# Attention outputs kept as features by tokens and scaled by rows from DRAM, and maxima transposed by VectorE

## The chip, the cores and the metric

One core of a Trainium2 chip runs the whole kernel. The metric is the device time of an execution in microseconds; lower is better. The engines are TensorE (PE, with its weight loads PEld), VectorE (DVE), ScalarE (ACT), GpSimd (POOL) and SyncE (SP), which issues most DMAs; GpSimd issues some. Each engine works through its own instructions in a fixed order, and waits on semaphores for the others.

## The reference

A transformer block over 2048 tokens of 576 features, with 32 heads of 18 features and a conditioned layer norm; all data is float32.

```python
q, k, v = qkv[0], qkv[1], qkv[2]
scores = jnp.einsum("bhqd,bhkd->bhqk", q, k) * scale
p = _softmax(scores, axis=-1)
o = jnp.einsum("bhqk,bhkd->bhqd", p, v)
return (lambda x, *d: x.transpose(*d))(o, 0, 2, 1, 3).reshape(B, S, D) @ wo
...
x = x + ga * _A_ref(h, A_wqkv, A_wo)
h = _layernorm(x, axis=-1) * (1 + cb) + sb
x = x + gb * _B_ref(h, B_w_gate, B_w_up, B_w_down)
```

`_B_ref` is a gated feed-forward net with 4608 hidden features: `(sigmoid(h w_gate) * (h w_up)) w_down`.

## The kernel before

After the projection of q, k and v, attention runs in 32 **units**. Unit u holds a pair of heads p = u % 16 for half = u // 16 of the tokens, 1024 queries. A unit goes through 16 tiles of 128 keys (kt), two at a time: such a pair of steps has eight score matmuls (keys by queries, so a probability tile has the keys on its partitions), eight exponentials on ACT (L1088) and eight value matmuls (L656) that sum up in the accumulator `o`. A column of ones beside the values gives the sum of the probabilities, so `o` holds for each of four (head, 512 queries) a block of 32 partitions: 18 features, and the sum in the 19th.

Softmax subtracts each query's maximum. It comes from a second set of score matmuls (queries by keys, L550), whose results VectorE reduces (L556, L561) and, for a part, ACT helps with (L559). Eight such maxima go with each pair of steps, for a later unit. At the end of a unit's maxima `nm` (L568) holds the negated maxima, 128 queries by 16. `spread` (L577) transposes it on PE (L581), splits it into a high and a low part (ACT L585, VectorE L586), and four DMAs on SP (L590, `q<-mrows`) write it as two more rows of that unit's queries `q`. A score matmul (L1084) reads these rows too, so the first scores of a unit wait for the DMAs. SP also loads the heads of later units (`load_heads`, L514 to L522) at the start of each unit.

`taken` (L668) copies a finished accumulator to `oT`. `outputs` (L676) transposes it on PE in four blocks (L683), copies that back (ACT L699), takes the reciprocal of the sums (VectorE L702), and multiplies on GpSimd (L705) into `Oa` or, for the second half, `big`: tokens by features. `project_o` (L754) then turns each tile of 128 tokens again (L772; L789 for the last 64 features), because the product with wo needs features on the partitions; evacuates it (L778), splits it (GpSimd L779, L780) and multiplies. These parts hang beside the steps of attention: the first half's rows from unit 15 (with loads of wo, layer norm and operand parts behind them, `first_rows`) to unit 27, the second half's from there on. A pair of steps that has such matmuls beside it is called heavy here; the others are light. Features 384 and up of the second half's tokens go to DRAM (`oend`) and are projected after attention in `last_rows` (transposes at L1526 and L1534).

The order of PE and ACT is the order of the program: `STEPS` spells it out for the two steps of a pair by letters (t a score, m and r and x maxima, A/B/V values, K `taken`, G a place for a projection part, O and S the transposes of the outputs and of the maxima). VectorE's, GpSimd's and SP's orders come from a list scheduler that starts from the program's order. On GpSimd, `down_parts` (L939) splits the weights of the down projection from unit 4 to unit 15, in blocks that are tied to the exponentials of the steps (`paced`, L931), so that they don't run ahead.

Of the kernel before, what the change touches and what calls it, by code (L numbers as in the profile page):

```python
# [23 lines left out]
P = 128  # L24
# [63 lines left out]
def tile_block(ctx, tc, x_in, wqkv, wo, w_gate, w_up, w_down, c_in, w_mod, out):  # L88
# [206 lines left out]
    oend = dram.tile([P, 8, D - DL], F32, name="oend")  # L295
# [230 lines left out]
    def maxima():  # L526
# [4 lines left out]
        for u in range(UNITS):  # L531
# [4 lines left out]
            for i in range(8 * n):  # L536
                if last is not None and i == (9 if u == 1 else 8):
                    if u == 1:
                        for _ in spread(*last):
                            pass  # L540
                    else:
                        state["spread"] = last
# [34 lines left out]
    def spread(qs, nm):  # L577

        n = HW // P
        tp = bank()[0 : 2 * n, 0:P]  # L580
        nc.tensor.transpose(tp, nm.rearrange("p h t -> p (h t)"), ident)  # L581
        yield
        mrows = small.tile([32 + 2 * n, P], F32R, name="mrows", bufs=1)
        parts = [mrows[32 * l : 32 * l + 2 * n] for l in range(2)]
        nc.scalar.copy(parts[0], tp)  # L585
        nc.vector.tensor_sub(parts[1], tp, parts[0].bitcast(F32))  # L586
        for h in range(2):
            for l, part in enumerate(parts):
                to = 64 * h + 3 * DH + l
                nc.sync.dma_start(  # L590
                    qs[to : to + 1, :].rearrange("l (t q) -> l t q", q=P).bitcast(F32),
                    part[n * h : n * (h + 1), :].bitcast(F32),
                )
# [40 lines left out]
    Os = [Oa]  # L634
# [33 lines left out]
    def taken():  # L668

        if "whole" in state:  # L670
            half, p, acc = state.pop("whole")
            oT = epool.tile([P, 512], F32, name="oT")
            nc.scalar.copy(oT, acc)
            state["end"] = (half, p, oT)

    def outputs():  # L676

        if "end" not in state:
            return
        half, p, oT = state.pop("end")  # L680
        tp = bank().rearrange("p (b q) -> p b q", q=P)
        for b in range(4):
            nc.tensor.transpose(tp[:, b, :], oT[:, b * P : (b + 1) * P], ident)  # L683

        yield
        tq = tp.rearrange("p b (j e) -> p j b e", e=32)
        rec = epool.tile([P, 4, 4], F32, name="rec")
        if half == 1 and p == H // 2 - 1:
            nc.vector.reciprocal(rec, tq[:, :, :, DH])
            state["last"] = epool.tile([P, 512], F32, name="oT")[:, 0 : 16 * DH].rearrange("p (t e) -> p t e", t=8)  # L690
            for h in range(2):
                nc.vector.tensor_tensor(
                    state["last"][:, :, h * DH : (h + 1) * DH].rearrange("p (c b) e -> p c b e", c=2),
                    tq[:, 2 * h : 2 * h + 2, :, 0:DH],
                    rec[:, 2 * h : 2 * h + 2, :].unsqueeze(3).to_broadcast([P, 2, 4, DH]),
                    op=ALU.mult,
                )
            return
        nc.scalar.copy(oT, tp.rearrange("p b q -> p (b q)"))  # L699
        yield  # L700
        tq = oT.rearrange("p (b j e) -> p j b e", j=4, e=32)
        nc.vector.reciprocal(rec, tq[:, :, :, DH])  # L702
        for h in range(2):
            f0 = (2 * p + h) * DH
            nc.gpsimd.tensor_tensor(  # L705
                Os[half][:, :, f0 : f0 + DH].rearrange("p (c b) e -> p c b e", c=2),
# [1111 lines left out]
```

## Time and profile before

| what | us |
|---|---|
| runs before: median (lowest to highest) of 3 | 2798.32 (2797.94 to 2798.35) |
| the profiled execution | 2804.88 |
| its span in the trace | 2803.1 |
| attention, from the first exponential to the end | 236.1 to about 1531.8 |
| a light unit, u5 | 38.3 |
| four heavy units, u16 to u19 | 183.7 |
| the gate, up and down stages behind attention | 1271 |

The page's first rows give an engine's busy time and its share of the span. In a group of instructions stand: line, engine, operation, output <- input, shapes and count, then the busy time in all, the mean of one in ns, and the idle time before with what ended it. In a timeline row the first number is the start, the second the time until the last of the counted instructions has ended; a row SPq or POOLq is an issue of a DMA. In a window row each engine has its busy time and count, and behind them the granted clock, the mean busy share of the DMA engines and GB/s.

### The profile page before, as it was taken

Reading aid. Unit: us, or ns where it says so; the run is one execution under the profiler, and the core shown is the slowest. Engines: PE = TensorE matmul, PEld = TensorE weight load, DVE = VectorE, ACT = ScalarE, POOL = GpSimd, SP = SyncE. Lnnn points to the kernel's source line nnn. Section 1 sums busy time; section 2 is a strip of 40 time slices with the busy share of each in tenths; the row PEclk is TensorE's granted clock in tenths of the full one; section 3 lists DMA queues with packets and bytes.
Section 4 is the critical chain, followed back from the end, with each engine's and each line's share of the span. In section 5 each row is a group of like instructions: output and inputs, shape, how many; then the busy total and the mean of one; then the engine's idle time right before and its main releaser. Section 6 shows DMA issues by size and latency. Waiting matters only on the chain.

```text
span 2803.1 us, 50644 instructions
## 1 busy us (share of the span) xinstructions
PE 2771.9 (99%) x18637; PEld 1847.4 (66%) x18637; DVE 2306.3 (82%) x4370; ACT 1609.3 (57%) x3051; POOL 814.6 (29%) x1077
## 2 busy tenths in 40 slices
PE   7999999999999999999999999999999999999999
PEld 5975444444444444444444888888888888888888
DVE  7278999999998888999883778888898677777777
ACT  3215999999999878999888332333333222222221
POOL 3125207888843111663103222232221100000000
PEclk9999999999999999999999999999999999999999
DMA  5344224444432120232127766667767956566653
GB/s 172 121 157 140 78 61 162 171 169 166 172 133 82 36 58 24 98 106 71 43 68 227 273 222 223 240 213 273 278 245 280 339 195 201 194 200 195 200 195 120
DMA packets 170777, 462.59 MB, mean 165 GB/s; under 512 B 21212, under 2 KB 88032, under 8 KB 160416
## 3 DMA queue, kind: packets, MB, share of 16 engines
q1 hardware_dynamic: 150064, 360.72, 38.4%
q0 software_dynamic: 20464, 98.62, 9.9%
q8 instruction: 147, 2.41, 0.4%
q14 instruction: 102, 0.84, 0.1%
HBM read 281.92 MB, written 176.82 MB: 164 GB/s over the span
## 4 chain that ended last, share of the span: by engine, by line
PE 92%; DVE 4%; DMA 2%; issue 2%; POOL 0%; ACT 0%; SPq 0%; DVEq 0%; ACTq 0%; POOLq 0%
PE x L1225 26%; PE o L656 19%; PE s L1084 12%; PE s L550 11%; PE d L1375 8%; PE d L1307 6%; PE s L336 4%; PE s L805 2%; PE s L389 1%; DMA out_dram<-Oa 1%; DVE mx L556 1%; PE s L683 1%; DMA wq_raw<-in_A_wqkv_dram 1%; DVE w L1215 0%; DVE Oa L1379 0%
## 5 line engine op out<-in xcount | busy, mean ns | idle before, releaser
L1088 ACT ACTIVATE p<-s 128x512 f32<-128x512 f32 x2048 | 1069.1, 616 | 89.2 <-PE s L1084 62.6
L556 DVE TENSOR_REDUCE mx<-s 128x1 f32<-128x512 f32 x1568 | 1000.9, 683 | 101.3 <-PE s L550 75.1
L656 PE MATMUL o<-p,vaug 128*32 128x256 f32 (+1 forms) x5848 | 595.1, 478 | 0.1
L550 PE MATMUL s<-k,q 54*128 54x512 f32 x1920 | 548.6, 434 | 2.0 <-DVE t L775 1.0
L1084 PE MATMUL s<-q,k 56*128 56x512 f32 x1920 | 527.7, 440 | 0.0
L550 PEld LDWEIGHTS s<-k,q 54*128 54x128 f32 x1920 | 273.4, 184 | 231.9 <-DVE mx L561 88.0
L1084 PEld LDWEIGHTS s<-q,k 56*128 56x128 f32 x1920 | 249.8, 184 | 232.1 <-ACT p L1088 72.9
L1225 PE MATMUL x<-k,w 128*128 128x512 f32 x1512 | 370.0, 392 | 0.0
L1225 PEld LDWEIGHTS x<-k,w 128*128 128x128 f32 x1512 | 276.8, 188 | 53.3 <-PE o L656 0.8
L1375 PE MATMUL d<-wd,hh 128*128 128x288 f32 x1248 | 249.9, 295 | 2.4 <-DVE Oa L1379 2.4
L656 PEld LDWEIGHTS o<-p,vaug 128*32 128x32 f32 x5848 | 116.2, 108 | 203.1 <-issue 187.5
L1225 PE MATMUL x<-big,w 128*128 128x512 f32 x1008 | 245.5, 392 | 0.7 <-DVE u L1724 0.7
L1225 PE MATMUL x<-w,w 128*128 128x512 f32 x1008 | 245.3, 391 | 0.0
L1225 PEld LDWEIGHTS x<-big,w 128*128 128x128 f32 x1008 | 185.1, 188 | 37.0 <-DVE u L1724 1.1
L1225 PEld LDWEIGHTS x<-w,w 128*128 128x128 f32 x1008 | 184.3, 188 | 34.5
L1375 PEld LDWEIGHTS d<-wd,hh 128*128 128x128 f32 x1248 | 202.2, 188 | 6.2 <-DVE Oa L1379 3.1
L1375 PE MATMUL d<-wd,hl 128*128 128x288 f32 x624 | 184.3, 295 | 0.0
L1379 DVE TENSOR_TENSOR Oa<-Oa,d 128x288 f32<-128x288 f32 x312 | 136.6, 453 | 55.1 <-PE d L1375 51.2
L561 DVE CUSTOM_DVE_ANT_0 over<-s,over 128x512 f32<-128x512 f32 x240 | 163.9, 683 | 1.3 <-PE s L1084 1.2
L559 ACT ACTIVATE over<-s 128x512 f32<-128x512 f32 x240 | 145.8, 608 | 11.3 <-PE s L550 9.3
L1234 ACT ACTIVATE sg<-x 128x512 f32<-128x512 f32 x36 | 21.6, 599 | 210.2 <-PE x L1225 210.2
L1206 ACT CAST w<-S 128x768 fp32r<-128x768 f32 x71 | 59.4, 836 | 137.8 <-POOL S L1179 136.0
(275 smaller groups left out, 3898.5 us busy)
## 6 DMA issues: line engine op xcount, KB each, us to landing
ws<-w SPq DMA_DIRECT2D x126, 640.0 KB
w<-ws SPq DMA_DIRECT2D x126, 640.0 KB
wd<-wds SPq DMA_DIRECT2D x19, 1152.0 KB
k<-kd SPq DMA_DIRECT2D x60, 360.0 KB
wds<-w POOLq DMA_DIRECT2D x18, 1152.0 KB, 5.2
wtd<-t POOLq DMA_DIRECT2D x32, 576.0 KB, 5.0
wt<-wtd SPq DMA_DIRECT2D x64, 288.0 KB
wd<-wds SPq DMA_DIRECT2D x52, 288.0 KB
```

What stands on the lines that cost most here:

```text
L336: nc.tensor.matmul(acc, w, hT[:, t, cols], start=n == 0, stop=n == len(ts_) - 1)
L550: nc.tensor.matmul(sp, qs[rows, qt * P : (qt + 1) * P], ks[rows, at * 512 : (at + 1) * 512], start=True, stop=True,)
L556: nc.vector.tensor_reduce(to, sp, axis=AX.X, op=ALU.max)
L559: nc.scalar.activation(over, sp, AF.Relu)
L561: nc.vector.tensor_tensor_reduce(out=over, in0=sp, in1=over, scale=1.0, scalar=LOWEST, op0=ALU.add, op1=ALU.max, accum_out=mx[:, h * n + q ...
L656: nc.tensor.matmul(acc[32 * j : 32 * j + 32, cols], vaug[:, kt, (2 * p + h) * VW : (2 * p + h) * VW + 32], probs[2 * c + h][:, cols], star ...
L1084: nc.tensor.matmul(sT, ks[rows, kcols], qs[rows, c * 512 : (c + 1) * 512], start=True, stop=True)
L1088: state["exp"] = nc.scalar.activation(pr, sT, AF.Exp, scale=SCALE)
L1225: nc.tensor.matmul(acc[v], w[:, v, a, :], X[s][:, b, :], start=first and n == 0, stop=n == 6, skip_group_check=not first,)
L1307: nc.tensor.matmul(acc, a[:, rows], w[:, k, :], start=n == 0, stop=n == 2)
L1375: nc.tensor.matmul(acc[:, :HALF], a[:, f, rows], w[:, f, cols], start=n == 0, stop=n == 5)
L1379: nc.vector.tensor_add(Oa[:, t, cols], Oa[:, t, cols], acc[:, :HALF])
```

## The change

`oT` stays features by tokens. Four small DMAs on SP lay the four rows of sums out as `sT` (128 partitions by 16), VectorE takes the reciprocal of that, one DMA stores it to `osums` in DRAM, and one loads it back as `R`, with each row of 512 repeated on 32 partitions. GpSimd multiplies `oT` by `R` in place, and four DMAs write the 18 features of each block to `ot` in DRAM, 576 features by 2048 tokens. `load_rows` brings tiles of 128 features by 1024 tokens back into `big`, which is then the operand of the projection with wo without a transpose: `project_rows` takes the place of `project_o`, with its splits (`rows_parts`) one tile of tokens ahead on GpSimd. The last unit's accumulator is stored unscaled to `lastd`, and `last_rows` scales it. `spread` splits the maxima first, transposes them with VectorE in blocks of 32x32, and eight DMAs write two rows at a time. The letters O and S leave `STEPS`, and a heavy pair is no longer held back at kt 2 and 12.

```diff
-    2: "V m1t0 t1t0 m0m1 O A c m1r0 t1m0 t1t0 G B c x0t1 m1t0",
-    4: "V r0m1 t1t0 m1m0 G A c t0t1 m1t0 B t1m0 m1t0 t1x0",
-    12: "V t0m1 m0t1 m1t0 S A c r0t1 m1t0 G B c t1t0 m1x0 t1m0",
 }
...
-    oend = dram.tile([P, 8, D - DL], F32, name="oend")
+    ot = dram.tile([D, S], F32, name="ot")
+    osums = dram.tile([UNITS, 4, 512], F32, name="osums")
+    lastd = dram.tile([P, 512], F32, name="lastd")
...
     def spread(qs, nm):
 
         n = HW // P
-        tp = bank()[0 : 2 * n, 0:P]
-        nc.tensor.transpose(tp, nm.rearrange("p h t -> p (h t)"), ident)
-        yield
...
+        split = small.tile([P, 4 * n], F32R, name="split", bufs=1)
+        hi, lo = (split.rearrange("p (h l t) -> p h l t", h=2, l=2)[:, :, l, :] for l in range(2))
+        nc.vector.tensor_copy(hi, nm)
+        nc.vector.tensor_sub(lo, nm, hi.bitcast(F32))
+        mrows = small.tile([P, 4 * n], F32R, name="mrows", bufs=1)
+        nc.vector.transpose(mrows.bitcast(F32), split.bitcast(F32))
+        for a in range(4):
+            for h in range(2):
+                to, p0 = 64 * h + 3 * DH, 32 * a + 2 * n * h
                 nc.sync.dma_start(
-                    qs[to : to + 1, :].rearrange("l (t q) -> l t q", q=P).bitcast(F32),
-                    part[n * h : n * (h + 1), :].bitcast(F32),
+                    qs[to : to + 2, :].rearrange("l (t a q) -> l t a q", a=4, q=32)[:, :, a, :].bitcast(F32),
+                    mrows[p0 : p0 + 2 * n, :].bitcast(F32),
                 )
...
     def taken():
+        if "whole" not in state:
             return
+        half, p, acc = state.pop("whole")
+        oT = epool.tile([P, 512], F32, name="oT")
+        nc.scalar.copy(oT, acc)
+        if half == 1 and p == H // 2 - 1:
+            nc.sync.dma_start(lastd, oT)
+            return
+        sT = epool.tile([P, 16], F32, name="sT")
+        for j in range(4):
+            one = oT[32 * j + DH : 32 * j + DH + 1, :]
+            nc.sync.dma_start(sT[32 * j : 32 * j + 32, :], one.rearrange("l (q r) -> l q r", r=16))
+        follow.append(outputs(half, p, oT, sT))
+
+    def outputs(half, p, oT, sT):
+
+        while state["kt"] < 2:
+            yield
+        rec = epool.tile([P, 16], F32, name="rec")
+        paced(nc.vector.reciprocal(rec, sT))
+        to = osums[half * H // 2 + p]
+        nc.sync.dma_start(to.rearrange("j (q r) -> (j q) r", r=16), rec)
+        R = state["room"] if "room" in state else bgp.tile([P, 512], F32, name="R")
+        nc.sync.dma_start(R, to.unsqueeze(1).to_broadcast([4, 32, 512]))
         yield
+        while state["kt"] < 6:
+            yield
+        paced(nc.gpsimd.tensor_mul(oT, oT, R))
         for h in range(2):
...
+            for c in range(2):
+                f0, n0, j = (2 * p + h) * DH, half * HW + c * 512, 2 * h + c
+                nc.sync.dma_start(ot[f0 : f0 + DH, n0 : n0 + 512], oT[32 * j : 32 * j + DH, :])
...
+    def load_rows(half, tiles):
+
+        own = slice(half * HW, (half + 1) * HW)
+        for i in tiles:
+            if i < 4:
+                nc.sync.dma_start(state["rows"][:, i, :], ot[i * P : (i + 1) * P, own])
+            else:
+                for p0 in (0, 64):
+                    nc.sync.dma_start(state["rows"][p0 : p0 + 64, 4, :], ot[DM:D, own])
+    def rows_parts(t):
...
+        src = state["rows"][:, 0:n, cols]
+        oh, ol = (T[:, a : a + n * P] for a in (0, 512))
+        oh3, ol3 = (a.rearrange("p (i q) -> p i q", q=P) for a in (oh, ol))
+        nc.gpsimd.tensor_copy(oh3, src)
+        nc.gpsimd.tensor_sub(ol3, src, oh3.bitcast(F32))
+        om = None
+        if t < 8:
+            om, omh = bgp.tile([P, P], F32R, name="om", bufs=2), T_[:, 640:768].bitcast(F32R)
+            end = state["rows"][:, 4, cols]
+            nc.gpsimd.tensor_copy(om[0:64], end[0:64])
+            nc.gpsimd.tensor_copy(omh[64:P], end[64:P])
+            nc.gpsimd.tensor_sub(om[64:P], end[64:P], omh[64:P].bitcast(F32))
+    def project_rows(t0):
+
+        ahead = rows_parts(t0)
+        if t0:
+            yield
...
+        for t in range(t0, t0 + 8):
+            n, oh, ol, om, xt = ahead
+            for h in range(2):
...
+                nc.vector.tensor_add(to[:, cols], xt[:, cols], acc[:, 0:HALF])
+                if h == 0 and t < t0 + 7:
+                    ahead = rows_parts(t + 1)
+                if h == 1 and t >= 8:
+                    nc.gpsimd.dma_start(x1p[:, t - 8, :], xt)
...
-        for t in range(8):
-            yield from project_o(t)
+        yield from project_rows(0)
...
+        if u in (14, 26):
+            state["big"] = big.tile([P, 8, 640], F32, name="big").rearrange("p a b -> p (a b)")
+            state["rows"] = state["big"].rearrange("p (i n) -> p i n", n=HW)
+            if u == 26:
+                state["room"] = state["big"][:, 4 * HW : 4 * HW + 512]
+            load_rows(u // 26, range(3) if u == 14 else range(2))
...
-                hold = heavy and (kt == 2 or kt == 12 and u < UNITS - 1)
-                halved = step >= 10 and (hold or not heavy)
+                halved = step >= 10 and not heavy
...
-                elif does in "OSG":
-                    if halved and kt == 2:
-                        follow.append(outputs())
-                        next(follow[-1], None)
+                elif does == "G":
                     if "spread" in state:
-                        follow.append(spread(*state.pop("spread")))
-                        next(follow[-1])
-                    if does == "G" and step >= FROM0 and not hold:
+                        spread(*state.pop("spread"))
+                    if step >= FROM0:
                         state["next"] = next(rows0 if step < FROM1 else rows1, None)
...
+            if (u, kt) == (15, 9):
+                load_rows(0, (3,))
+            if (u, kt) == (16, 7):
+                load_rows(0, (4,))
+            if (u, kt) == (27, 7):
+                load_rows(1, (2,))
...
+                c = t0 // 4
+                n0 = HW + 512 * c
+                od = pool.tile([P, 2, 512], F32, name="od")
+                nc.sync.dma_start(od[:, 0, :], ot[DL:DM, n0 : n0 + 512])
...
+                for p0 in (0, 64):
+                    p1 = p0 + 64 - 2 * DH
+                    nc.sync.dma_start(end[p0:p1], ot[DM : D - 2 * DH, n0 : n0 + 512])
+                    for h in range(2):
+                        j, p2 = 2 * h + c, p1 + h * DH
+                        nc.sync.dma_start(end[p2 : p2 + DH], lastd[32 * j : 32 * j + DH, :])
+                        nc.sync.dma_start(R[p2 : p2 + DH], to[j : j + 1, :].to_broadcast([DH, 512]))
...
+                nc.vector.tensor_mul(end, end, R)
```

The lists below are the instruction order of an engine in the compiled program; names are tiles, and a number behind x counts like rows in a run.

SP in unit 4 and around it. Before, with the maxima's rows as `mrows`:

```order
L518 DMA k_2233<-kd 36x1x2560
L522 DMA k_2233<-kd 18x2560
L198 DMA gates<-w_4052 1x288 x2
L199 DMA gb_b<-gates 128x576
L590 DMA q_1029<-mrows 1x8x128 x4
L514 DMA q_1021<-qd 36x1x1024
```

The same engine now, in unit 5; `sT` are the sums, `ot` the outputs in DRAM:

```order
L521 DMA k_2242<-kd 18x2560
L677 DMA sT<-oT 32x1x16 x4
L687 DMA osums<-rec 128x16
L689 DMA R<-osums 128x1x512
L697 DMA ot<-oT 18x512 x4
L587 DMA q_1027<-mrows 2x8x32 x8
L513 DMA q_1031<-qd 36x1x1024
L516 DMA q_1031<-qd 18x1024
L517 DMA k_2236<-kd 36x1x2560
L521 DMA k_2236<-kd 18x2560
```

The rows of maxima stood alone among loads, and now stand behind the seven DMAs of the outputs, whose last four wait for GpSimd's product.

GpSimd in unit 5, where `w` and `t` are tiles of the down weights and `wtd` their place in DRAM. Before:

```order
L992 DMA wtd<-t_5478 128x1152
L990 CAST t_5479<-t_5479 128x288
L943 DMA w_5793<-in_B_w_down_dram 128x2x576
L991 TENSOR_TENSOR t_5479<-t_5479 128x288
L992 DMA wtd<-t_5479 128x1152
L964 TENSOR_TENSOR w_5443<-w_5443,gb_b 128x288 x3
L973 TENSOR_TENSOR t_5836<-w_5443 128x288
L960 CAST w_5443<-w_5443 128x288 x2
```

And now, at the same place:

```order
L979 DMA wtd<-t_5524 128x1152
L977 CAST t_5525<-t_5525 128x288
L930 DMA w_5848<-in_B_w_down_dram 128x2x576
L978 TENSOR_TENSOR t_5525<-t_5525 128x288
L979 DMA wtd<-t_5525 128x1152
L693 TENSOR_TENSOR oT<-oT,R 128x512
L951 TENSOR_TENSOR w_5492<-w_5492,gb_b 128x288 x3
L960 TENSOR_TENSOR t_5891<-w_5492 128x288
```

The product of the outputs stands between two blocks of the down weights; the two products of L705 of that unit stood ahead of the first of them.

VectorE now, near the end of a light unit's maxima; `mx` are maxima, an ISA row with a tile `over` is the two-input maximum:

```order
L685 RECIPROCAL rec<-sT 128x16
L554 TENSOR_REDUCE mx_1042<-s_4985 128x1
L554 TENSOR_REDUCE mx_1042<-s_4988 128x1
L554 TENSOR_REDUCE mx_1042<-s_4999 128x1
L554 TENSOR_REDUCE mx_1042<-s_5016 128x1
L559 ISA over,mx_1042<-s_5023,over 128x512
L559 ISA mx_1042 128x1
L554 TENSOR_REDUCE mx_1042<-s_5034 128x1
L566 TENSOR_REDUCE nm<-mx_1042 128x16
L580 CAST split<-nm 128x2x8
L581 TENSOR_TENSOR split<-nm,split 128x2x8
L554 TENSOR_REDUCE mx_1041<-s_5047 128x1
```

The reciprocal stood a pair of steps after the copy of `oT` (L699) before; it now stands six maxima ahead of `nm`, and the split of the maxima directly behind it. The transposes of `split` (L583) follow four reduces later.

More of the change, by code (lines that the diff above doesn't have):

```diff
@@ L538, in maxima @@
                     if u == 1:
-                        for _ in spread(*last):
-                            pass
+                        spread(*last)
                     else:
@@ L748, in load_wo @@
         weights.extend((wo_h, wo_l, we))
[L749 removed]
+        for _ in range(6):
             yield
     held_rows = []
[L754 to L810 removed]
@@ L995, in down_parts @@
                     yield
-    def last_rows_project():
-        for t in range(8, NT):
-            yield from project_o(t)
     def load_block(pool, b, k, tied=None):
@@ L1133, in tile_block @@
     taken()
-    for _ in outputs():
-        pass
     manual.close()
-    nc.sync.dma_start(oend[:, :, D - DL - 2 * DH :], state["last"])
     att.close()
@@ L1518, in last_rows @@
             nc.gpsimd.dma_start(w, wod)
[L1519 to L1526 removed]
+            sT = pool.tile([P, 16], F32, name="sT")
```

160 lines of the change are left out of this document (40 added, 120 removed).

## The prediction

> **What bounds the kernel now.** First the page: busy shares, then the chain that ended last.
>
> ```profile
> span 2803.1 us, 50644 instructions
> PE 2771.9 (99%) x18637; PEld 1847.4 (66%) x18637; DVE 2306.3 (82%) x4370; ACT 1609.3 (57%) x3051; POOL 814.6 (29%) x1077
> PE 92%; DVE 4%; DMA 2%; issue 2%; POOL 0%; ACT 0%; SPq 0%; DVEq 0%; ACTq 0%; POOLq 0%
> ```
>
> PE is busy for 99% of the span, but that is an average over stages. So next come the windows: one light unit of attention (u5, no projection beside it), four heavy ones (u16 to u19, with project_o), the two matmul pairs of one t of project_o in u18 and the whole t of four pairs, one t in u29, and all that follows attention.
>
> ```profile
> core 0: us, PE busy (x) PEld busy (x) DVE busy (x) ACT busy (x) POOL busy (x), PEclk, DMA share, GB/s
> 435.33:473.61 38.28, 38.28 (x329) 16.53 (x329) 35.66 (x68) 37.43 (x77) 28.78 (x47) 1.00 0.56 196
> 856.72:1040.38 183.66, 182.97 (x1413) 87.34 (x1405) 158.09 (x314) 151.59 (x300) 34.19 (x62) 1.00 0.17 50
> 962.18:968.70 6.52, 6.52 (x50) 3.54 (x46) 4.91 (x10) 4.65 (x11) 0.00 (x0) 1.00 0.00 0
> 968.70:975.66 6.96, 6.92 (x51) 3.58 (x47) 5.66 (x12) 5.11 (x10) 0.86 (x2) 1.00 0.09 15
> 962.18:986.11 23.93, 23.70 (x182) 11.66 (x178) 20.47 (x42) 18.72 (x38) 3.78 (x7) 1.00 0.05 14
> 1419.13:1436.65 17.52, 17.00 (x127) 7.88 (x125) 15.19 (x29) 13.97 (x27) 1.12 (x2) 1.00 0.11 37
> 1531.80:2803.00 1271.20, 1262.77 (x6946) 1112.96 (x6942) 1017.48 (x1901) 355.20 (x567) 173.94 (x172) 1.00 0.66 228
> ```
>
> In the light unit ACT is busy 37.4 of 38.3 us and VectorE 35.7: these two set it, and PE's "busy" is full because matmuls wait inside it. In the heavy units and after attention the work of PE itself does. So what leaves PE is worth its time in heavy pairs and at the end, and little in light pairs.
>
> **What is removed.** The groups by line, and under them one line of the up stage:
>
> ```profile
> L683 PE MATMUL s<-ident,oT 128*128 128x128 f32 x128 | 20.9, 286 | 0.1
> L699 ACT COPY oT<-s 128x512 f32<-128x512 f32 x31 | 20.5, 662 | 0.0
> L585 ACT CAST mrows<-s 16x128 fp32r<-16x128 f32 x32 | 7.7, 239 | 0.0
> L586 DVE TENSOR_TENSOR mrows<-s,mrows 16x128 fp32r<-16x128 f32 x32 | 9.0, 280 | 4.4 <-ACT mrows L585 3.4
> L702 DVE RECIPROCAL rec<-oT 128x16 f32<-128x16 f32 x31 | 7.8, 252 | 15.8 <-ACT oT L699 15.4 <-issue 0.4
> L705 POOL TENSOR_TENSOR Oa<-oT,rec 128x144 f32<-128x144 f32 x32 | 13.1, 431 | 97.8 <-DVE rec L702 97.6
> L780 POOL TENSOR_TENSOR t<-t,t 128x384 fp32r<-128x384 f32 x4 | 4.0, 1010 | 0.3
> ...
> L1526 PE MATMUL d<-ident,od x8: 272/272/273, 1559.9 to 1624.2; 128*128 128x128 f32 x8
> ```
>
> In a light unit ACT loses L699 and L585, 0.9 us. VectorE loses L586 (0.28) and gets a copy, a subtraction and a 32x32 transpose of 16 or 32 columns; the trace has no such transpose, so I price the three by the small rows here, 0.22 to 0.28 each: +0.4 to +0.6 us. VectorE, already close, then holds the unit at about 38.0: **-0.3** (bounds 0 and -0.9, all of ACT's share). Over the eleven light units without a new wait (u1 to u4, u14, u15, u21, u22, u24 to u26): -3.5.
>
> Heavy pairs: a t of project_o took 23.93 us for four pairs, two of them with transposes only; the new form has two matmul pairs a t (6.52 and 6.96 here; the longer one holds transposes' evacuations beside it) and frees two, which fall back to a light pair's 4.75 (38.28 / 8). 8 x (2 x 6.5 + 2 x 4.75) = 180.0 against the 186.3 that the same 32 pairs took (u16 pair 3 to u20 pair 2): **-6** (bounds -2.5 with the mean of the two, 6.74, and -10 with 6.25 for it if the evacuations' waits go as well). The second half's 17.52 for three pairs, 5.84 each, becomes 2 x 5.84 + 4.75 = 16.43: -8.7 at most for eight, of which I take **-3**, as three of the eight t run beside held pairs. Five more units are in part PE's (u0, u22, u23, u30, u31) and lose 4 x 0.286 of L683 and 0.28 of L581, 1.4 us each: -7 at most, **-4** taken, as about half of their pairs are light. After attention the eight transposes of L1526 and as many of L1534, 272 ns each, leave a stage that PE bounds: **-4** (0 to -4.4), with new small DMAs on SP hidden behind the up and gate work. Sum of the gains: **-20.5**.
>
> **What is added: the row chain on SP.** Now the question is what is late next. SP issues in program order, and the first listing of the change shows its order in a unit: sT, osums, R, four stores of ot, and only then the eight mrows, which the next unit's first scores read. The first ot store waits for GpSimd's product. Before, four issues of mrows followed VectorE and nothing stood ahead of them:
>
> ```profile
> 387.19 2.75 SPq L590 DMA_DIRECT2D q<-mrows  x4
> 395.57 2.06 ACT L1088 ACTIVATE p<-s 128x512 f32<-128x512 f32 x4
> 458.90 0.22 DVE L568 TENSOR_REDUCE nm<-mx 128x16 f32<-128x64 f32 x1
> L198 SPq DMA_DIRECT2D gates<-w x4: 221/229/252, 325.1 to 403.6; - x4
> 406.31 0.36 SPq L199 DMA_DIRECT2D gb_b<-gates  x1
> 330.54 0.35 SPq L199 DMA_DIRECT2D ga_b<-gates  x1
> ```
>
> The issues took 0.69 each and ended at 389.94; the next unit's first exponential ran at 395.57, so there was room. In the new order, with m the time in the unit at which the product starts: 1.28 for the product (L857 below), four stores x 0.65, eight rows of which the last starts 7 x 0.69 later, 1.75 until it has landed (no row shows it: an estimate, two thirds of the 2.7 that the gates below took until a load could follow, since this store ends on the chip), and 0.72 from first score to first exponential. So a unit can't be shorter than **m + 11.2** (1.28 + 2.6 + 4.85 + 1.75 + 0.72). A unit of 38.2 needs m at or below 27.0.
>
> What sets m? First R. By the third listing five reduces and one two-part maximum stand between RECIPROCAL and nm, 3.4 to 4.0 us (0.22 to 0.28 for the small rows is not among them; a reduce is 0.683 by its group below, a little less where they overlap); nm ran at 458.90, u5 + 23.6, so the reciprocal runs at 19.6 to 20.3. Then the store to DRAM and the load that waits for it: the last gates store was issued at 403.6 and the load that waits for it went at 406.31, 2.7 us later; with 0.25 for the reciprocal and 2.3 to 2.8 for the load of R, R is there at u + 24.9 to 26.1. That just fits, with one or two microseconds to spare.
>
> Second, GpSimd's own order. The second listing shows that in u5 the product stands behind the whole block of the down weights up to L992. In the trace of before the row behind which it stands ran here, in u5 to u13:
>
> ```profile
> 435.33 1.08 ACT L1088 ACTIVATE p<-s 128x512 f32<-128x512 f32 x2
> 468.54 0.56 POOL L992 DMA_DIRECT2D wtd<-t  x1 [0.30 <-POOL t L991]
> 502.41 0.59 POOL L984 DMA_DIRECT2D wds<-w  x1
> 540.35 0.42 POOL L990 CAST t<-t 128x288 fp32r<-128x288 f32 x1
> 578.96 0.56 POOL L992 DMA_DIRECT2D wtd<-t  x1 [0.30 <-POOL t L991]
> 623.06 0.72 POOL L943 DMA_DIRECT2D w<-in_B_w_down_dram  x1 [2.15 <-DMA wds<-w]
> 659.67 0.81 POOL L991 TENSOR_TENSOR t<-t 128x288 fp32r<-128x288 f32 x1
> 693.33 0.56 POOL L992 DMA_DIRECT2D wtd<-t  x1 [0.30 <-POOL t L991]
> 737.68 0.56 POOL L992 DMA_DIRECT2D wtd<-t  x1 [0.30 <-POOL t L991]
> 770.66 0.59 POOL L984 DMA_DIRECT2D wds<-w  x1
> ```
>
> Units start 38.3 apart from 435.33, so these rows end at 33.8, 29.4, 28.9, 29.4, 35.1, 33.5, 28.6, 34.6 and 29.4 in their units: 282.7 in all. Less 0.8 each, since the two products of L705 are gone: 282.7 + 9 x (11.2 - 0.8) = 376.3 against 9 x 38.3 = 344.8. In u6 and u13 one row stands ahead of the stores, -0.7 each. That makes **+30** (bounds 0, if GpSimd catches up, and +38, if its blocks also shift). While PE waits there, ACT and VectorE wait with it, and nothing covers it.
>
> The same in u23, where the product is listed behind an operand part of the normalised rows:
>
> ```profile
> 1258.79 1.28 POOL L857 TENSOR_TENSOR t<-t 128x512 f32<-128x512 f32 x1 [0.70 <-DVE t L917]
> 1278.21 0.56 POOL L854 DMA_DIRECT2D xs<-ho  x1
> ```
>
> That stretch took 20.0 us. In the new order it starts behind a transposed block some 18.6 into the unit, so m = 38.0 after the removed work, the unit 49.2 against about 40.2: **+9** (bounds 0 and +12). I place that block by the order, behind four pairs of 4.65. In u27 the first projection waits for rows of ot that SP loads behind the stores (L744). By the order it stands behind 6.5 pairs of 4.9, at 31.8; the stores are issued by 26.1 + 1.3 + 2.6 = 30.0, half a megabyte at the light unit's 196 GB/s takes 2.7 and 1.75 to land, GpSimd's copy and subtraction (L780) 0.5 + 1.0: 35.9, **+4** (0 to +6). u16 by the same reading **+2.3** (0 to +4), u15 +0.3. Sum of the waits: +46.
>
> **Sum.** 46 - 20.5 = **+25.6 us**: 2804.88 of the profiled execution becomes 2830.5. The runs' median, 2798.32, lies 6.6 us below that execution, and the prediction is a median: 2798.3 + 25.6 = **2824**.
>
> **The rivals.** GpSimd's waits from 435 to 830 decide the first:
>
> ```profile
> POOL w L943 <- DMA wds<-w: 37.3, 16, 6.4
> POOL w L964 <- ACT p L1088: 20.5, 8, 4.3
> ```
>
> (a) *GpSimd reaches the product in time*: 37.3 us of its holes wait for its own stores, not for attention, and a unit that is stretched hands it that time; if m stays below 27.0 in u5 to u13, u23 and u27, all 46 us go and the gains stay: 2798.3 - 20.5 = 2778, faster. Against it: eight blocks of the sixteen start only when an exponential lets them (20.5 us), so they shift with the units. The point of decision is m = 27.0. (b) *R itself is late in every light unit*: the other gates, first issued at 325.1, could be loaded only at 330.54: 5.2 us after the second store, in place of 2.7. With 2.5 more, 1.0 of it covered, eleven light units get 1.5 each: 2841; with the sums' first load and store as slow too, 2862. I give it 2848. The light unit's row shows DMA engines busy at 0.56, the heavy ones' 0.17, which speaks for slow trips just there. The Trainium skill, "DMA: Bandwidth & Descriptors", section "Latency and other measured facts", says that reaching DRAM takes 0.2 us on average and 2 us under high load; by that figure, as an estimate, two trips could add 3.6 us a unit, and eleven units at 2.6 beyond the cover would give 2853. The two waits in this trace, 2.7 and 5.2, agree with such a spread, and no run here shows it with its load. (c) *GpSimd catches up in part*: with 2.3 us less before each product (37.3 / 16) the nine units lose 9 x 2.3 = 21 of their 30, and 25 stand against -20.5: 2803, no change.
>
> **How the numbers follow.** Chances: forecast 0.60 (own range 2808 to 2840), a 0.15, b 0.16, c 0.09. A measurement of this kernel tells apart about 0.2%, 5.6 us. Slower: 0.60 and 0.16, less a little: 0.74; same 0.09; faster 0.17. The range leaves out a and the top of b: 2792 to 2856.
>
> **What would show it.** In the changed profile SP's waits name GpSimd's oT before the ot stores; ACT's exponentials pause just at the starts of u6 to u14 and u24, released by PE's scores, and PE's scores by the DMA of mrows; units there are 39 to 45 us, u1 to u4 and u14 near 38. Heavy pairs run one after the other at 6.5, and the chain's share of L683 is gone. Wrong would be: units of 38 in u5 to u13 (a), or 39.5 in all light units with R as the releaser of GpSimd (b).

## The result, and the profile after

| | us |
|---|---|
| runs after: median (lowest to highest) of 4 | 2892.69 (2888.06 to 2894.94) |
| runs before beside them: median of 4 | 2798.13 (2795.52 to 2798.35) |
| ratio, with its 95% interval | 1.0338 (1.032 to 1.0356): slower |
| span of the profiled execution, before and after | 2803.1 and 2885.9 |

Slower, as forecast, but by 94.6 us in place of 25.6. The page after, its first rows, the granted clock and the chain:

```profile
span 2885.9 us, 51086 instructions
PE 2774.4 (96%) x18397; PEld 1833.7 (64%) x18397; DVE 2305.5 (80%) x4406; ACT 1593.9 (55%) x2988; POOL 831.0 (29%) x1048
...
PEclk9999999998988999999999999999999999999999
...
PE 82%; DVE 5%; DMA 4%; POOL 4%; issue 2%; SPq 2%; ACT 0%; DVEq 0%; POOLq 0%; ACTq 0%
```

PE is idle for 4% of the span, GpSimd, DMAs and SP stand on the chain, and the clock has holes in the part where the down weights are split. The groups removed are gone, 240 matmuls fewer, and yet PE's busy time is no smaller (2774.4 us against 2771.9); the rest is in waits. By stage, from the first exponential of each unit (us):

| | start | u0 | u1-u4 | u5-u13 | u14-u15 | u16-u20 | u21-u26 | u27-u31 | rest |
|---|---|---|---|---|---|---|---|---|---|
| before | 236.1 | 43.0 | 156.3 | 344.8 | 76.6 | 230.9 | 236.1 | 208.0 | 1271.3 |
| after | 233.5 | 41.1 | 161.5 | 403.4 | 95.4 | 234.8 | 241.7 | 208.9 | 1265.6 |

Of the 82.8 us between the two spans, 58.6 lie in u5 to u13 and 18.8 in the two units behind. One such unit, u5: SP's, GpSimd's and ACT's timeline of the changed kernel around its end. A name in brackets is what the engine waited for, with the idle time:

```profile
474.40 1.83 SPq L697 DMA_DIRECT2D ot<-oT  x4
476.33 5.38 SPq L587 DMA_DIRECT2D q<-mrows  x8
...
470.64 0.72 POOL L930 DMA_DIRECT2D w<-in_B_w_down_dram  x1 [2.69 <-DMA wds<-w]
...
473.07 1.30 POOL L693 TENSOR_TENSOR oT<-oT,R 128x512 f32<-128x512 f32 x1
...
483.03 1.81 ACT L1071 ACTIVATE p<-s 128x512 f32<-128x512 f32 x3 [7.99 <-PE s L1067]
```

The product starts 37.0 us into u5 (436.1), behind the block of down weights; SP holds the stores and, behind them, the eight rows; u6's first exponential comes 9.96 after the product's start, 7.99 of it as idle time of ACT. So the mechanism of the forecast is there. What it did not have is in PE's clock over the same place:

```profile
476.00:478.00 2.00, 0.00 (x0) 0.00 (x0) 0.00 (x0) 0.00 (x0) 2.00 (x4) 1.00 0.19 46
478.00:480.00 2.00, 0.00 (x0) 0.00 (x0) 0.00 (x0) 0.00 (x0) 2.00 (x5) 0.60 0.02 3
480.00:482.00 2.00, 0.00 (x0) 0.00 (x0) 0.00 (x0) 0.00 (x0) 1.92 (x4) 0.50 0.02 3
482.20:484.20 2.00, 1.97 (x8) 0.97 (x12) 0.48 (x1) 1.05 (x2) 2.00 (x4) 0.50 0.18 50
484.20:486.20 2.00, 2.00 (x16) 0.54 (x10) 0.57 (x2) 0.95 (x3) 2.00 (x4) 0.50 0.49 113
486.20:488.20 2.00, 2.00 (x16) 0.99 (x14) 1.73 (x4) 0.96 (x3) 2.00 (x5) 0.50 0.90 307
488.20:490.20 2.00, 2.00 (x16) 0.59 (x14) 1.20 (x3) 1.97 (x4) 1.69 (x3) 0.89 0.95 270
```

Behind each engine's busy time stands the granted clock. PE's last matmul ended by 474.6; some 4 us later the clock falls to 0.50, and it is back only some 6 us after PE has work again. In that stretch the first pair of u6 takes 7.29 us, where it takes 4.33 behind no wait. Over all of attention the mean granted clock is 0.96, where it was 1.00. The Trainium skill, "TensorE: Matmul & The Clock Gate", section "Part 1: The HAM clock gate", says that PE falls to half its clock after an idle window of about 3.4 us and is released after as long a busy one; the fall here, behind an idle time of 7.8 us, agrees, the way back took nearly twice that.

And VectorE's split of the maxima, in the changed kernel's rows of that line, and at its worst place in u2:

```profile
L580 DVE CAST split<-nm x32: 165/176/5217, 208.9 to 1576.7; 128x16 fp32r<-128x16 f32 x32
...
337.33 5.22 DVE L580 CAST split<-nm 128x16 fp32r<-128x16 f32 x1
342.59 0.17 DVE L581 TENSOR_TENSOR split<-nm,split 128x16 fp32r<-128x16 f32 x1
...
337.04 2.77 POOL L140 TENSOR_TENSOR big<-big 128x576 f32<-128x576 f32 x2
339.77 2.75 POOL L140 TENSOR_TENSOR big<-big,w 64x576 f32<-64x576 f32 x2
```

A copy that takes 0.17 us takes 5.22 while GpSimd runs four operations in a row, and ends with the last of them. That is a second thing that the forecast did not have.

### The profile page after: what moved, and what is told of

The parts are those of the page before. It is cut to its first block, busy times and chain, and to the rows that moved or that the text cites. A ratio compares the mean times of both kernels' runs of the same rounds, so it can differ in the third digit from the quotient of the medians.

```text
span 2885.9 us, 51086 instructions
## 1 busy us (share of the span) xinstructions
PE 2774.4 (96%) x18397; PEld 1833.7 (64%) x18397; DVE 2305.5 (80%) x4406; ACT 1593.9 (55%) x2988; POOL 831.0 (29%) x1048
## 4 chain that ended last, share of the span: by engine, by line
PE 82%; DVE 5%; DMA 4%; POOL 4%; issue 2%; SPq 2%; ACT 0%; DVEq 0%; POOLq 0%; ACTq 0%
PE x L1209 27%; PE o L652 15%; PE s L1067 10%; PE s L548 8%; PE d L1359 8%; PE d L1291 6%; PE s L335 3%; PE s L791 2%; DVE mx L554 2%; PE s L388 1%; DMA wds<-w 1%; SPq L587 1%; POOL w L951 1%; POOL w L948 1%; DMA q<-mrows 1%
## 5 line engine op out<-in xcount | busy, mean ns | idle before, releaser
L1067 PE MATMUL s<-q,k 56*128 56x512 f32 x1920 | 549.2, 451 | 70.1 <-DMA q<-mrows 50.8
L652 PE MATMUL o<-p,vaug 128*32 128x256 f32 (+1 forms) x5848 | 610.0, 488 | 0.2 <-ACT oT L670 0.2
L548 PE MATMUL s<-k,q 54*128 54x512 f32 x1920 | 566.7, 447 | 0.0
L1067 PEld LDWEIGHTS s<-q,k 56*128 56x128 f32 x1920 | 258.1, 190 | 337.9 <-issue 123.7
L548 PEld LDWEIGHTS s<-k,q 54*128 54x128 f32 x1920 | 283.2, 189 | 219.7 <-DVE mx L559 66.2
```

The lines of the kernel that those rows point to most:

```text
L548: nc.tensor.matmul(sp, qs[rows, qt * P : (qt + 1) * P], ks[rows, at * 512 : (at + 1) * 512], start=True, stop=True,)
L652: nc.tensor.matmul(acc[32 * j : 32 * j + 32, cols], vaug[:, kt, (2 * p + h) * VW : (2 * p + h) * VW + 32], probs[2 * c + h][:, cols], star ...
L1067: nc.tensor.matmul(sT, ks[rows, kcols], qs[rows, c * 512 : (c + 1) * 512], start=True, stop=True)
```

## The experiments

The kernel before took 2797.5 to 2799.4 us beside these runs, as the median. e2 and e3 were run once, the others four times or more. Units are the distances of first exponentials, from ACT's rows.

**e1: the stores of ot on GpSimd's queue**, so that SP has nothing that waits for the product.

```diff
-                nc.sync.dma_start(ot[f0 : f0 + DH, n0 : n0 + 512], oT[32 * j : 32 * j + DH, :])
+                nc.gpsimd.dma_start(ot[f0 : f0 + DH, n0 : n0 + 512], oT[32 * j : 32 * j + DH, :])
```

> The changed kernel, but the four stores of ot a unit are issued by GpSimd, behind its own product; nothing on SP waits for the product any more. Theory A (the maxima's rows wait on SP behind the stores that wait for GpSimd): u5 to u15 and u23 fall from 41 to 52 us a unit to 37.8 to 38.5 and PE's waits for q<-mrows go; the clock that PE loses after such a wait comes back too; 2892.7 - 61 (u5 to u13) - 19 (u14, u15) - 9 (u23, u24) = about 2803. The waits of u16 and u27 for rows of ot stay. Rival B (the rows are late by themselves: eight small DMAs, or R through DRAM): the units stay at 41 to 48 and the time above 2870.

2853.24 us, ratio 1.0204 (1.0182 to 1.0225): 39 faster than the change, and far from the 2803 of A. PE's waits in attention, of the change and then of this run:

```profile
PE s L1067 <- DMA q<-mrows: 50.8, 10, 11.2
```

```profile
PE s L1067 <- issue: 18.4, 1, 18.4
PE o L652 <- ACT oT L670: 16.1, 3, 7.1
PE s L1067 <- DVE mx L554: 14.9, 12, 3.7
```

The wait for the rows is gone, as A says, and u5, u7, u8, u11, u12, u14 take 37.7 to 38.7. But the product is still late, and its lateness comes out elsewhere: ACT's next copy into `oT`, of which there is one, waits for the stores that read it (u6 46.2, u13 47.2). In u15 SP's load of `big<-ot` stands ahead of three of the rows and waits for the stores; u9 and u10 take 43.5 and 44.5, where VectorE's split is held for 3.5 and 4.0. So the place on SP was one part of the matter; the late product itself was another. A second buffer for `oT` was not tried.

**e2: the high part by a second reduction.**

```diff
-        nc.vector.tensor_copy(hi, nm)
+        nc.vector.tensor_reduce(hi, mx.rearrange("p (h t) c -> p h t c", h=2), axis=AX.X, op=ALU.max, negate=True)
```

> The changed kernel, but the high part of the maxima is written by a second reduction of mx in place of a copy of nm. In the changed kernel that copy took 0.17 us where GpSimd was idle and 5.22 in u2, where it ended with the fourth of four GpSimd operations in a row; the reduction nm itself never took over 0.25. Theory A (this kind of copy is held while GpSimd computes, a reduction isn't): the row of L580 takes about 0.2 everywhere and u2 is 5 us shorter, unless the subtraction behind it is held for as long. Rival B (any small operation there is held, by something else in u2): the reduction takes 5 us in u2 too. The whole time: 2885 to 2893 by A, unchanged by B.

2871.13 us. The reduction took 0.21 everywhere. In u2 it was the subtraction behind it that now took 5.12, so u2 stayed at 46.35. So the hold is not of one instruction but of a kind: A holds, with the subtraction held in the copy's place. The subtraction has two inputs in SBUF. The time lies below the 2885 to 2893 of A; why u5 to u13 came to 387.0 in place of 403.4, a single run does not tell.

**e3: late rows in the kernel before.**

```diff
+    HOLD = {6: 4, 7: 8, 8: 12, 9: 16, 10: 20, 11: 6, 12: 10}
...
+        for _ in range(HOLD.get(late["u"], 0)):
+            nc.sync.dma_start(spare[late["n"]], parts[1][0:n, :].bitcast(F32))
+            late["n"] += 1
```

> The kernel before, with 4, 8, 12, 16, 20, 6 and 10 extra stores of 4 KB on SP between the first and the second of the four rows of maxima of u6 to u12; 0.63 us each, so 2.5, 5.0, 7.6, 10.1, 12.6, 3.8 and 6.3 us later rows; about 3.8 us of that had room. Nothing else is changed. Theory A (a wait of PE at a unit's start costs itself and a lower granted clock behind it): u6 and u11 stay at 38.3; u7, u12, u8, u9, u10 wait 1.2, 2.5, 3.8, 6.3, 8.8; behind a wait of about 3 us and more the first pair of the next unit is some 3 us longer than 4.36 with a granted clock of 0.5, behind the short ones it isn't. Rival B (the long first pairs of the changed kernel come from its loads of the next heads, late behind the rows on SP, or from its new orders): here too those loads are late, but no granted clock falls, or the first pairs grow with the lateness of the loads also where PE hardly waited.

2818.23 us. The stores were quicker than thought, 0.35 to 0.71 us each in the mean of a unit, so the lateness is less. PE's waits in this run, and the clock in two-microsecond windows behind the longest (at the start of u11, with 20 stores in u10):

```profile
PE s L1091 <- DMA q<-mrows: 10.5, 5, 6.1
```

```profile
676.50:678.50 2.00, 1.88 (x11) 0.70 (x11) 0.69 (x1) 1.62 (x3) 0.00 (x0) 0.50 0.52 176
680.50:682.50 2.00, 2.00 (x16) 0.84 (x9) 1.66 (x4) 1.25 (x3) 0.00 (x0) 0.50 0.58 195
682.50:684.50 2.00, 2.00 (x14) 0.68 (x14) 0.69 (x2) 1.40 (x3) 0.51 (x1) 0.75 0.56 176
684.50:686.50 2.00, 2.00 (x20) 1.06 (x18) 1.88 (x3) 1.91 (x4) 2.00 (x4) 1.00 0.16 44
```

PE waited 2.96 us at the start of u10 and 6.11 at that of u11; both times the clock fell to 0.50, and the first pairs took 8.79 and 8.08 us, against 4.36. The waits at u7 and u9, 0.86 and 0.63 us, left the clock at 1.00. The heads' loads behind the rows come later here too, but no wait of PE names one; so the long first pairs go with the clock: PE waited 10.5 us, u5 to u13 grew by 20.2 (365.0 against 344.8). In this run the waits cost about twice their length.

**e4: the maxima alone**, in the kernel before: `spread` of the changed kernel, all else as it was.

```diff
-                        follow.append(spread(*state.pop("spread")))
-                        next(follow[-1])
+                        spread(*state.pop("spread"))
```

> The kernel before with the new way of the maxima alone (split, 32x32 transposes by VectorE, eight DMAs); the outputs stay tokens by features. Theory A (this part is not what costs): ACT loses 0.24 us a unit and PE a transpose, VectorE gets about 0.3; 2790 to 2800, u2 some 5 us longer if the copy is held there by GpSimd as in the changed kernel. Rival B (the eight DMAs of 128-byte pieces make the rows late): light units above 38.3 with PE waiting for q<-mrows, 2815 or more.

2826.19 us, ratio 1.0101 (1.0084 to 1.0118): +28.7, and neither theory as it was put. No unit waits for the rows. The loss is VectorE's: u2 46.1, u22 46.7 and u25 44.5, which took 39.7, 40.3 and 39.8 before, and u5 to u13 +7.6. Part of it is again the clock: behind PE's waits in u2, u22 and u25 (3.9, 4.1 and 1.6 us) it stood at 0.50 for 6.8 us each.

```profile
L581 DVE CAST split<-nm x32: 160/175/4216, 210.0 to 1508.0; 128x16 fp32r<-128x16 f32 x32
L582 DVE TENSOR_TENSOR split<-nm,split x32: 161/175/3530, 210.2 to 1508.2; 128x16 fp32r<-128x16 f32 x32
```

**e5: the outputs alone**: the changed kernel with `spread` as before.

> The changed kernel with the maxima's rows made as before (PE transpose, ACT copy, VectorE subtraction from PSUM, four DMAs); the outputs stay features by tokens. Theory A (two separate losses: the outputs' product late on GpSimd, some 75 us, and the maxima's split held on VectorE while GpSimd computes, 28.7 us when the maxima are changed alone): 2892.7 - 28.7 = 2864, up to 15 us less since four rows are issued in place of eight behind the product (2.8 us a late unit); u2 falls from 46.6 to about 39; u15 and u16 stay above 50. Rival B (the losses are one, and the outputs alone cost nothing or gain): 2780 to 2810.

2862.45 us, ratio 1.0231 (1.0217 to 1.0246), as A put it (2864). u2 is back at 39.6; u15 takes 49.9 and u16 53.2. Each against the kernel before beside it, the two halves cost 28.7 and 63.0, together 91.7 of the 94.6: they nearly add up.

**e6: the product ahead in GpSimd's order.** On e5: each later operation of the down weights, of wo, of the rows' and the operand parts is tied behind the last product.

```diff
+    def behind(op):
+
+        if "mul" in state:
+            tc.add_manual_dep(
+                op.ins, state["mul"].ins.name,
...
-                nc.gpsimd.tensor_copy(hi[:, quads[i]], raw[:, quads[i]])
+                behind(nc.gpsimd.tensor_copy(hi[:, quads[i]], raw[:, quads[i]]))
```

> As the run with the outputs alone, and GpSimd's later parts (down weights, wo, operand parts) are tied behind the product once the product is written, so that the product stands ahead of them in GpSimd's order; R still comes at 27 us in a unit, and GpSimd waits for it. Theory A (the stall is the product's place in GpSimd's order): the product starts at 27 to 28 us in u5 to u13, u15 and u23, these units take 37.5 to 38.5, PE's waits for q<-mrows go and the granted clock is back at 0.99; the time falls to 2780 to 2800, less what GpSimd's blocks lose by their wait (if they run late, u15 and u16 pay: up to 2815). Rival B (the rows are late through R, the DMAs or SP's crowding): units stay at 41 and more, above 2840.

2837.64 us, ratio 1.0139 (1.012 to 1.0157), above A's range and just below B's. u5 and u9 take 37.7, u15 37.9 in place of 49.9. But GpSimd waits 8.2 us for R in u5 and lacks that time afterwards: the product starts at 36.3 in u7, 34.6 in u10, 33.0 in u11. A product that waits for an R that is there at 27, on an engine that is nearly full, comes late elsewhere.

**e7: the sums early.** On e6: `load_heads(u + 2)` is written behind kt 1.

```diff
-        if 0 < u < UNITS - 2:
-            load_heads(u + 2)
...
+            if kt == 2 and 0 < u < UNITS - 2:
+                load_heads(u + 2)
```

> As the run with the product ahead, and the loads of the heads of unit u + 2 are written behind kt 1, so that SP issues the sums' small DMAs sooner and VectorE takes the reciprocal about 28 rows earlier, near 10 us in the unit; R is there near 16. Theory A: GpSimd no longer waits long for R, its blocks are on time, the rows of ot for u16 and u27 are there in time: 2770 to 2785, faster than both kernels. Rival B (the later loads of the heads make the maxima of unit u + 2 wait, which read them from pair 5 on): light units of 40 and more with PE waiting for k<-kd or q<-qd.

2809.76 us, ratio 1.0033 (1.0021 to 1.0045): 28 better, yet slower than before and above A's range. From u3 on the products start at 18 to 27, and no unit waits for the rows any more. VectorE waits in their place: its reciprocal stands so early that the sums are not there.

```profile
DVE rec L697 <- DMA sT<-oT: 21.5, 9, 5.1
```

**e8: the maxima alone, split from PSUM.** On e4: the maxima are reduced into a PSUM bank and split from there.

```diff
-            nm = small.tile([P, 2, n], F32, name="nm")
+            nm = bank()[:, 0 : 2 * n]
+            nc.vector.tensor_reduce(nm, mx, axis=AX.X, op=ALU.max, negate=True)
...
+            nc.vector.tensor_copy(hi, nm)
+            nc.vector.tensor_sub(lo, nm, hi.bitcast(F32))
```

> The run with the maxima alone, except that the negated maxima are reduced into a PSUM bank and split from there, so that the copy has no SBUF input and the subtraction only one. Theory A (VectorE's copy and subtraction are held because they read SBUF while GpSimd computes): both rows take 0.16 to 0.30 us everywhere, u2 is back from 46.1 to about 39.5 and u5 to u14 from 39.1 to 38.0 to 38.3; 2826.2 - 28.7 = about 2797, between 2790 and 2802. Rival B (the 32x32 transposes, the eight DMAs or the wider rows cost the time): 2815 and more. Rival C (the wait is at the output in SBUF, not at the inputs): the two rows stay long, 2820 to 2826.

2818.26 us, ratio 1.0072 (1.0059 to 1.0086). The rows of the two lines, the copy and the subtraction:

```profile
L571 DVE CAST split<-s x32: 165/174/176, 205.6 to 1499.6; 128x16 fp32r<-128x16 f32 x32
L572 DVE TENSOR_TENSOR split<-s,split x32: 164/165/175, 206.4 to 1499.8; 128x16 fp32r<-128x16 f32 x32
```

No hold is left, u2 takes 39.95, and u5 to u13 346.7 in place of 352.4; with u22 and u25 that is 20.7 us less than in e4. So the hold is of inputs in SBUF; the output `split` lies there in both. The time did not follow (A put 2797), since PE now waits for VectorE to read the bank: u16 to u20 grow from 230.3 to 240.7, and one pair of u18 takes 10.2, where e4 has 5.6. PE in that pair, and the clock behind it:

```profile
980.56 1.11 PE L769 MATMUL s<-ident,Oa 128*128 128x128 f32 x4 [1.59 <-DVE split L572]
...
980.33:983.74 3.41, 3.18 (x16) 1.42 (x16) 1.11 (x5) 0.23 (x1) 1.12 (x2) 0.50 0.03 7
983.74:987.16 3.42, 3.42 (x20) 1.23 (x22) 2.31 (x5) 2.35 (x6) 0.76 (x1) 0.50 0.02 3
```

So here a wait of 1.6 us was enough for 6.8 us at half the clock.

**e9: all mended**: the changed kernel with the split from PSUM, the ties and late heads' loads of e6 and e7, and, in most units, the reciprocal at kt 6 and the product at kt 8.

> The changed kernel with the split from PSUM, the heads' loads behind kt 1, the reciprocal written at kt 6 and the product at kt 8 (two kt sooner in u16 and u27), and GpSimd's later parts tied behind the product. Theory A (the product's place, the sums' late chain, the held split and the lost clock are the whole loss): no unit waits for the maxima's rows, light units take 37.7 to 38.0, u17 and u18 52.0 and 51.1, granted clock 0.99 or more; 2809.8 of the run before it less 22 (its pair 2 waits for the sums) less some 8 (PE transposes in heavy pairs): 2770 to 2785, faster than both kernels. Rival B (something else in the new form costs, such as crowded DMAs): above 2800 with light units over 38.5.

2814.99 us, ratio 1.0068 (1.0055 to 1.008): A's number missed. u5, u6, u13, u14 take 37.7, but in u7 to u12 the product starts at 27.3 to 33.4 and u5 to u13 take 359.8; behind u30, which grew to 42.6, PE waited 7.4 us for the rows. How much of the rest is the PSUM bank's, as in e8, stays open.

**e10: the sums between.** On e7: the reciprocal at kt 4, and VectorE's maxima (split in SBUF) only where GpSimd has little beside them, in u16 to u18 and from u27.

```diff
-        while state["kt"] < 2:
+        while state["kt"] < 4:
...
+                        if 16 <= u <= 18 or u >= 27:
+                            spread_dve(*state.pop("spread"))
```

> The run with the sums early, but the reciprocal is written at kt 4, some six rows later in VectorE's order (it waited 21.5 us in all for the sums there, at 7.7 to 10.8 us in a unit), and in u16 to u18 and from u27 on, where GpSimd had nothing beside it, the maxima are split and transposed by VectorE in place of PE. Theory A (what was left in that run were VectorE's wait for the sums and PE transposes in heavy pairs): pair 2 of u5 to u14 is back at 4.65, -20; u17 at 52 and u28 at 47, -8: 2809.8 - 28 = about 2782, faster than the kernel before by 10 to 18. Rival B (GpSimd's blocks are late then and the product with them): units of 39 to 43 somewhere in u5 to u14, 2795 to 2805.

2785.78 us, ratio **0.9961 (0.9947 to 0.9974): faster than the kernel before**, by 12.5 us, near A's 2782. The window of u5 to u13, of the change and then of this run:

```profile
436.11:839.52 403.41, 362.00 (x2879) 148.97 (x2876) 327.71 (x622) 335.75 (x659) 285.40 (x444) 0.92 0.48 166
```

```profile
429.83:772.82 342.99, 341.43 (x2893) 145.62 (x2894) 321.38 (x604) 333.05 (x668) 272.84 (x422) 1.00 0.55 186
```

Nearly the same GpSimd work (272.84 us in place of 285.40) fits in 60 us less, with the clock at 1.00. All of these units but u7 take 37.7 to 37.8; in u7, 41.0, the reciprocal waits 1.7 us, PE 1.6 behind it, and the clock falls for 3.4.

## Why the prediction was right and wrong

The direction, the chain of waits on SP and the place in GpSimd's order were right. The forecast of 2824 was wrong in its size. Put the gains at the forecast's 20.5, and the 82.8 between the spans leaves about 103 us of losses where 46 were forecast. (The waits as listed add up to 45.6; the half microsecond does not matter.)

- *The gains, -20.5.* A light unit without a wait takes 37.72 (u3) against 38.27: -0.55, where -0.3 was taken. Heavy pairs run one behind the other at 6.5 (u17: 52.0 for eight). For what comes after attention -4 was taken; 1271.3 became 1265.6, but e3, e4 and e8, which keep the kernel before there, took 1266.7 to 1269.1, so what of the -4 came is not shown. e10, which has few waits left, is ahead of the kernel before by 12.5 us in the medians, with some 3 us left in u7. It keeps PE's transposes of the maxima in most units, so the 20.5 was neither reached nor refuted.
- *m + 11.2.* Measured m + 9.96 in u5: the four stores took 1.83 or less, not 2.6. Over u5 to u13 it is m + 9.2 to 12.9, 95.8 in sum, where nine times 11.2 are 100.8. R came at 27.1 (u3, the product's start), a microsecond behind the range of 24.9 to 26.1, and still fit: its load was issued 1.7 behind the reciprocal, not 2.95, but then took 5.3, not 2.3 to 2.8. The one error covers part of the other. The 1.75 for the landing of a row no run shows by itself. Rival b, R late in every light unit, did not occur; of the late units only u11 and u14 waited for R by more than half a microsecond (7.0 and 8.4).
- *The product's place, +30 in u5 to u13.* These units grew by 58.6. In the forecast's own sum the whole surplus is m: the nine products started at 307.6 us in sum, where 275.5 was read off the trace of before (282.7 less 0.8 each), 32 more, against 5 less behind them. That is past the +38 that was put for shifted blocks. GpSimd's waits from 430 to 885, where the trace of before had 37.3 for its stores and 20.5 for exponentials, tell what moved the blocks:

```profile
POOL w L951 <- ACT p L1071: 57.0, 11, 11.3
POOL w L930 <- DMA wds<-w: 51.2, 14, 7.8
```

- ***The step that failed first: "While PE waits there, ACT and VectorE wait with it, and nothing covers it".*** It took the price of a wait to be its length. The first pairs of u6 to u14 are 25.8 us longer in sum than 4.33, while PE's clock is at 0.50, and e3 shows the same without the rest of the change; no term of the sum had it. Not all of this counts, since a unit ends some 10 us behind its product, whatever its first pair took. It counts where the product's place hangs on ACT or VectorE. In u6, u7, u10 and u13 the block ahead of the product waits for an exponential (the first row above), and the exponentials come late behind the long first pair: the four pairs are 13.0 longer, the four products 13.7 later than put. In u11 the first pair is 5.1 longer, the reciprocal and R come as much later, and the product 6.5. So some 20 of the 32 go with the clock. This is a reading of the trace: no run changes the clock alone in the new kernel. In u5, u8, u9 and u12 (11.9 in sum) GpSimd's blocks wait for its own stores instead (the second row): there, as far as the rows tell, the long first pair counts for nothing. The waits for stores, 2.3 us in the mean before, are 3.7.
- The trace of before had a sign of it. The windows that the forecast quotes show the clock at 1.00, but at the start of attention, behind a wait of PE of 0.94 us, it is at 0.50 for 6.8 us, and the first pair of u0 takes 6.53 against the 4.36 of later units. (The same wait had it in seven of this case's twelve traces; u0 takes 41.6 to 45.0 in these and 40.0 to 41.1 in the others, the change among them.)

```profile
241.10:243.10 2.00, 2.00 (x10) 0.83 (x6) 0.89 (x2) 0.48 (x1) 1.10 (x2) 0.50 1.12 304
```

- ***The second: the three small rows at "+0.4 to +0.6 us" a unit.*** Their bare times were right (0.17, 0.17, 0.20). They were priced by rows that GpSimd didn't touch; beside GpSimd the copy and the subtraction took up to 5.22, and alone this half of the change costs 28.7 us (e4). e8 shows what it is: the same two operations from PSUM take 0.17 throughout, and the units that had grown are 20.7 shorter.
- ***The third: u15 at +0.3.*** The product stood behind the parts of wo there, each of which waits 2.6 to 6.8 us for its load, and started at 40.5: u15 took 52.1 against 38.3. u14, where the product waited for R and started at 34.0, took 43.3. With the product tied ahead (e6), u15 takes 37.9.
- *u23, u27 and u16.* u23's product started at 38.2 (38.0 put) and the unit took 47.8 (49.2 put). In u27 and u16 PE waited 6.0 and 6.5 us for rows and for `om`, and part of it for the clock again; +4 and +2.3 were put.

Rival a, that GpSimd reaches the product in time, fell: the stretched units did not hand it the time, as its waits for its own stores and for exponentials grew with them.

## What to carry to other kernels

A queue that issues in program order joins everything in it: before a DMA with a wait is put ahead of others, ask what stands behind it and where its releaser stands in that engine's own order. Price a wait of the matrix engine of some 2 us or more at its length and, where its pairs set the time, another 3 to 5 us behind it; shorter ones may cost this too (e8). A small operation's row holds only beside the same neighbours: look what GpSimd does at that moment, and feed VectorE from PSUM, or keep it for stretches in which GpSimd rests.

## What the runs showed of the hardware that was not expected

VectorE's copy and its subtraction of two SBUF tiles waited for the end of GpSimd's running operation (0.17 became 0.3 to 1.3 us) and sometimes through several in a row: 5.22 us over four in u2. A reduction (0.21 to 0.22), the reciprocal (0.24 to 0.26) and the 32x32 transposes (0.19 to 0.22) beside the same work did not, nor the copy and subtraction out of PSUM. The Trainium skill, "GPSIMD Engine Reference", section "8. Key points", says that GpSimd shares SBUF interfaces with VectorE, in contention with VectorE's operations in a two-port mode or with two SBUF inputs. e2, e4 and e8 agree for the subtraction, which has two SBUF inputs, and is spared when one is in PSUM; whether the copy runs in a two-port mode no run here shows. They add that the wait can span several operations.

In the light units of the changed kernel, PE's clock came back 5 to 10 us after PE had work again, behind waits of 2.4 to 7.8 us; it stood at 0.50 for 3.4 us (u15), 6.8, 10.2 or 13.7. The first pair behind such a wait was 2.6 to 5.1 us longer than 4.33 (u6, u7, u9 to u11, u13, u14). A longer wait did not make it longer: in e3 it was 4.4 behind 2.96 us and 3.7 behind 6.11. In the twelve traces of this case every wait of PE in attention of more than 1.6 us had the clock at 0.50 around its end or within 5 us behind it; of those from 0.9 to 1.6 us some had (1.59 in u18 of e8), some had not.
